# Float32r passes on split operands for the sine half of a dense layer, and the order of the steps around them

## The chip, the cores and the metric

The kernel runs on one core of a Trainium2 chip. The metric is the device time of one execution in microseconds (us). The kernel before takes 1928.28 us, the median of 3 runs (1928.05 to 1929.04).

## The reference

```python
X = np.fft.fft(x, axis=1)            # x: 8 x 3008 x 256, f32
X = np.fft.fft(X, axis=2)
x = X.real.astype(np.float32).reshape(24064, 256)
h = x @ w_in                         # 256 x 2048
g = h * np.clip(h + 3.0, 0.0, 6.0) / 6.0
out = g @ w_out                      # 2048 x 256
```

A Fourier transform over the sequence and over the features, of which the real part is kept, and then two dense layers with a hard swish between them.

## The kernel before

The Fourier transform over the sequence is done as 3008 = 47 x 64: `stage1` (47) and `stage2` (64) are matrix products with tables. The transform over the features is folded into the weights of the first dense layer. Because the input is real, rows k and -k share their products: with u the cosine half of the first layer and v the sine half, the layer's result is u + v for one row and u - v for its mirror row.

The batch of 8 is worked on in 4 pairs. A pair has 12 chunks of 256 columns (the last of each pair has 194, and 192 in the second layer); the features of the dense layers are taken in 8 groups `fc` of 256. One chunk and one `fc` make a step, so there are 4 x 12 x 8 = 384 steps. The first 8 also prepare the weights. The order of all instructions is written out by hand: the loop over steps at the end emits them, and each engine runs its own in that order. `beside` has lists of extra work by step, `ahead` (stage 2, loads, the spreading of a row to all partitions) and `behind` (stage 1).

In a step `s`, the loop emits

- `mlp1` of step s+2. `mlp1_products` (L546) makes four f32 products on TensorE, two for u and two for v, each 128 x 256, into two banks of PSUM. `activate` (L560) follows: on VectorE two operations (L565) add a rank-one term to u and put the sum into s; one makes u = s + v (L575), one v = v - s (L577). ScalarE makes a ReLU of each (L604), and VectorE the product with the upper clip (`gate`, L607) for each. The gated values are in tile a.
- `combine` of step s+1 on GpSimd (L621): sums of parts of a, into c. The second layer uses seven products for a 2 x 2 block product in place of eight.
- every chunk, `finish` (GpSimd) and `store` (transposes on VectorE, L712, and stores on SP's queue) of the chunk before.
- `mlp2` of step s (L651): seven f32 products on TensorE, three on parts of a, then four on c, added over the 8 groups into four banks. At the last group ScalarE copies them out (L661).

`activate_last` is `activate` for the short chunks. PSUM has 8 banks: 4 for the second layer (`ps_a`), 3 for u and v (`ps_h`) and one for the stages (`ps_d`). The tables T of stage 2 (six groups) are all kept in SBUF. `stage2` ends with a copy by ScalarE (L508), `spread` with two DMAs on SP's queue (L515, L516), `stage1` with two copies by ScalarE and DMAs on SP's queue.

Of the kernel before, what the change touches and what calls it, by code (L numbers as in the profile page):

```python
# [12 lines left out]
F16 = mybir.dt.float16  # L13
AL = mybir.AluOpType
# [34 lines left out]
WS = 2.0 ** 20  # L49
N1, N2 = 47, 64  # L50
# [8 lines left out]
def kernel(  # L59
# [41 lines left out]
    gpool = ctx.enter_context(tc.tile_pool(name="gpool", bufs=2))  # L101
    qpool = ctx.enter_context(tc.tile_pool(name="qpool", bufs=3))
# [4 lines left out]
    ps_d = ctx.enter_context(tc.tile_pool(name="ps_d", bufs=1, space=PSUM))  # L107
    ps_h = ctx.enter_context(tc.tile_pool(name="ps_h", bufs=3, space=PSUM))
    ps_a = ctx.enter_context(tc.tile_pool(name="ps_a", bufs=4, space=PSUM))

# [11 lines left out]
    T = consts.tile([P, 2, NG, 2, 2 * KK, N2], F32, name="T")  # L122
# [140 lines left out]
    def bank(shape, name):  # L263
        if starting[0]:
            return ps_a.tile(shape, F32, tag="acc", name=name)
        return ps_d.tile(shape, F32, tag="d", name=name)

    def stage1(pr, c):  # L270
        y = pr.y[c]
        ps = [bank([P, 2, D], "ps1"), ps_h.tile([P, 2, D], F32, tag="uv", name="ps1")]
        for h in range(2):
            last = (c, h) == (NXC - 1, 1)
            for b in range(2):
                n = 1 if last else 2
                nc.tensor.matmul(ps[b][h * PB:(h + 1) * PB, 0:n], F[rows(b), 0:PB], y[rows(b), 2 * h:2 * h + n],  # L277
                                 start=True, stop=not last, skip_group_check=last)
# [93 lines left out]
    def stage1_quarters(hb, m):  # L372
        y = hb.y.pop(m)
        cosine, sine = slice(0, P + 1), slice(P + 1, D)
        ps = [bank([P, 2, D], "ps1"), ps_h.tile([P, 2, D], F32, tag="uv", name="ps1")]
# [65 lines left out]
    def both_tables(gr, blk, u, tab=None):  # L441
        if tab is not None:
            return tab[:, gr, blk, u]
        t = T[:, :, gr, blk, 2 * u]
        (p, b, k), step = t.ap, T[:, 0, gr, blk, 2 * u:2 * u + 2].ap[1][0]
        return bass.AP(t.tensor, t.offset, [p, [b[0] + step, b[1]], k])
# [26 lines left out]

    def spread_half(hb, gr):
# [6 lines left out]
        nc.sync.dma_start(out=first.qn[vg][:, cs], in_=qd[:, cs].to_broadcast([P, TB]))  # L481
        del hb.g[gr]

    def spread_by_pe(hb, ps, tab, copy=nc.scalar.copy):
# [4 lines left out]
        copy(first.qn[0][:, 0:TB], ps)  # L489
        del hb.g[0]  # L490

    def stage2(pr, gr, i, copy=nc.scalar.copy):
# [5 lines left out]
        for u in range(2):  # L498
# [4 lines left out]
            for blk in range(2):  # L503
# [3 lines left out]
                                 T[:, :, gr, blk, kk, 0:nk], start=True, stop=True)  # L507
# [3 lines left out]
    def spread(pr, gr):  # L511
# [4 lines left out]
        nc.sync.dma_start(out=pr.qn[gr][:, 0:n], in_=qd[:, 0:n].to_broadcast([P, n]))  # L516
        del pr.g[gr]

    class Chunk:
# [3 lines left out]
        def __init__(self, pr, ck):  # L523
# [7 lines left out]
            self.a, self.c, self.acc = {}, {}, {}  # L531
# [28 lines left out]
    def activate(ch, fc, u, v, between=None):  # L560
# [11 lines left out]
        if ch.last:  # L572
            activate_last(a, t, s, u, v, nq)
            return
        nc.vector.tensor_tensor(u[:], s[:], v[:], op=AL.add)  # L575
        relu(t[:, 0], u[:], 1.0 / 6.0)
        nc.vector.tensor_tensor(v[:], v[:], s[:], op=AL.subtract)  # L577
# [8 lines left out]
    def activate_last(a, t, s, u, v, nq):  # L586
        un, vn, sn, tn = u[:, :, 0:nq], v[:, :, 0:nq], s[:, :, 0:nq], t[:, :, :, 0:nq]
        nc.vector.tensor_tensor(un, sn, vn, op=AL.add)
        relu(tn[:, 0], un, 1.0 / 6.0)
        nc.vector.tensor_tensor(vn, vn, sn, op=AL.subtract)  # L590
        relu(tn[:, 1], vn, -1.0 / 6.0)

        def slots(x, n, i):
            return x[:, i * P:i * P + 2 * n].rearrange("p (b k) -> p b k", b=2)

        gate(a[:, 0, :, 0:P], tn[:, 0, :, 0:P], u[:, :, 0:P])
        for f in range(2):
            gate(slots(a[:, 0, f], N2 // 2, 1), *(slots(x, NH, 1)[:, :, 0:NH - 1] for x in (t[:, 0, f], u[:, f])))
        for f in range(2):
            gate(slots(a[:, 1, f], N2, 0)[:, :, ::-1], *(slots(x, N2, 0) for x in (t[:, 1, f], v[:, f])))  # L600
            gate(slots(a[:, 1, f], N2 // 2, 1)[:, :, ::-1], *(slots(x, NH, 1)[:, :, 1:NH] for x in (t[:, 1, f], v[:, f])))

# [22 lines left out]
    def mlp2_first(ch, fc, halves=(0, 1)):  # L625
        a = ch.a[fc]
        for h in halves:
# [5 lines left out]
            if fc == NF - 1:  # L633
                if h == 0:
                    ch.r = epool.tile([P, 2, 2, TB], F32, tag="r", name="r")
# [3 lines left out]
    def mlp2(ch, fc):  # L639
        a = ch.a.pop(fc)[:].rearrange("p m f n -> p (m f) n")[:, :, 0:ch.n]  # L640
        c = ch.c.pop(fc)
        moving = [a[:, 0], a[:, 1], a[:, 3], c[:, 0], c[:, 1], c[:, 2], c[:, 3]]
        order = list(enumerate(moving))
        if ch.final and fc == NF - 1:

            order[5:] = order[:4:-1]
        for i, mv in order:
# [5 lines left out]
            if fc == NF - 1 and (i % 2 == 1 or i == 6):  # L653
                if i == 1:
                    ch.e = epool.tile([P, 8, TB], F32, tag="e", name="e")
# [7 lines left out]
    def finish(ch):  # L663
# [4 lines left out]
        r = epool.tile([P, 2, 2, TB], F32, tag="r", name="r")  # L668
# [9 lines left out]
    def finish_final(ch):  # L678
# [3 lines left out]
        ch.r = epool.tile([P, 2, 2, TB], F32, tag="r", name="r")  # L682
# [165 lines left out]
    def load_t(gr):  # L848
        nc.sync.dma_start(out=T[:, :, gr].rearrange("p b a k n -> p b (a k n)"), in_=c_stage2[gr])
# [147 lines left out]
    def beside(p):  # L997
# [7 lines left out]
        if p == 0:  # L1005
            for gr in range(2, NG):
                put(gr if gr < NSG else gr + 8, load_t, gr)
            for gr in range(2):
                put(14 + gr, load_t, gr)
# [23 lines left out]

        def s2(t, pr, gr):
            for i in range(2):
                put(t + 3 + 4 * i, stage2, pr, gr, i)
            put(t + 8, spread, pr, gr)
# [5 lines left out]
        if p + 1 < NP:  # L1043
            nx = pairs[p + 1]
            for c in range(NXC):
# [4 lines left out]
                put(t + 8, stage1, nx, c, at=behind)  # L1050
            put(NST * (NG - 1) - 2, load_g, nx, 0)
# [4 lines left out]
    def close_w():  # L1056
        nonlocal epool
        wctx.__exit__(None, None, None)
        epool = ctx.enter_context(tc.tile_pool(name="epool", bufs=2))

    epool = None
    steps = [(p, ck, fc) for p in range(NP) for ck in range(NCK) for fc in range(NF)]
    AHEAD = 2
# [100 lines left out]
    for s, (p, ck, fc) in enumerate(steps):  # L1164
# [12 lines left out]
        else:  # L1177
            if s + AHEAD < len(steps):
                mlp1(*chunk(s + AHEAD))
            for f, a in behind.get(ck * NF + fc, ()):  # L1180
                f(*a)
# [7 lines left out]
            mlp2(*chunk(s))  # L1189
# [5 lines left out]
def _tables(B, S, D):  # L1195
# [49 lines left out]
    t[0, -1], t[1, -1] = 1.0, (-1.0) ** np.arange(N2)  # L1245
    h = D // 2
# [47 lines left out]
```

## Time and profile before

| | |
|---|---|
| median of 3 runs | 1928.28 us |
| span of the profiled execution | 1926.0 us |
| TensorE busy (PE) | 1912.2 us, 99% |
| weight loads (PEld) | 1653.3 us, 86% |
| VectorE (DVE) | 1432.2 us, 74% |
| ScalarE (ACT) | 678.0 us, 35% |
| GpSimd (POOL) | 1447.7 us, 75% |
| granted TensorE clock | full in all 40 slices |

The profile is of one execution; its instructions and transfers are shown with times from the start of the span. The page has the busy time of each engine, and the chain of waits: the work that ended last, followed back through what released each piece of it. A timeline lists instructions in order of time, equal neighbours merged: start, time from the first start to the last end, engine, line, operation, out<-in, shape, count, and in brackets the idle time before with what ended it. A row by line gives the count, the busy time and the mean time of one. One f32 product on TensorE is two instructions in the profile, each with a weight load of its own. A matmul's record lasts from its start to its result, so that records of neighbours overlap; the rate is read from starts.

### The profile page before, as it was taken

What the parts mean: (1) busy time and instruction counts of PE and PEld (TensorE: products, weight loads), DVE (VectorE), ACT (ScalarE), POOL (GpSimd) and SP (SyncE); (2) the same over time, 40 slices, a digit from 0 to 9 for tenths busy, and PEclk for the clock granted to TensorE, in tenths of its full rate; (3) what the DMA queues carried; (4) which work ended last, traced back from release to release, by engine and by line L of the source; (5) the groups of instructions that cost most, each with busy time, mean ns of one, the idle gap of its engine ahead of it and who ended that gap; (6) DMA issues with size and microseconds to landing.
All of it is one profiled execution on the core that took longest, in us unless ns stands there. A gap on an engine that the chain in (4) does not pass through costs nothing.

```text
span 1926.0 us, 28448 instructions
## 1 busy us (share of the span) xinstructions
PE 1912.2 (99%) x9456; PEld 1653.3 (86%) x9456; DVE 1432.2 (74%) x2756; ACT 678.0 (35%) x1164; POOL 1447.7 (75%) x1658
## 2 busy tenths in 40 slices
PE   9999999999999999999999999999999999999998
PEld 6688888888988888888898888888899888888887
DVE  8967776777877777777787777777778777777777
ACT  6533333333333333333333333333333333333332
POOL 5697888896688788786678787878676667666765
PEclk9999999999999999999999999999999999999999
DMA  7442222211112212121111121221110101101000
GB/s 264 118 132 54 73 72 65 59 47 43 25 43 70 56 46 55 44 58 39 23 40 50 49 56 44 55 56 44 36 28 20 29 17 28 33 12 29 19 20 20
DMA packets 155258, 99.78 MB, mean 52 GB/s; under 512 B 121776, under 2 KB 135579, under 8 KB 155111
## 3 DMA queue, kind: packets, MB, share of 16 engines
q1 hardware_dynamic: 142854, 60.75, 12.9%
q0 software_dynamic: 11008, 36.63, 6.6%
q8 instruction: 74, 1.21, 0.3%
q10 hardware_dynamic: 1248, 0.59, 0.1%
q14 instruction: 74, 0.60, 0.1%
HBM read 61.44 MB, written 36.79 MB: 51 GB/s over the span
## 4 chain that ended last, share of the span: by engine, by line
PE 94%; POOL 2%; DVE 2%; issue 1%; ACT 1%; DMA 0%; SPq 0%; DVEq 0%; POOLq 0%; ACTq 0%
PE acc L651 56%; PE v L556 16%; PE u L556 16%; PE ps L505 2%; PE acc L631 1%; PE ps L277 1%; POOL c L621 1%; DVE a L607 1%; PE spare L832 0%; POOL xt L176 0%; DMA C<-in_c_dim_dram 0%; DVE s L565 0%; DVE o L712 0%; ACT t L604 0%; PE ps L466 0%
## 5 line engine op out<-in xcount | busy, mean ns | idle before, releaser
L621 POOL TENSOR_TENSOR c<-a 128x512 f32<-128x512 f32 (+1 forms) x375 | 469.6, 1252 | 357.8 <-PE acc L651 302.5
L651 PE MATMUL acc<-c,G 128*128 128x256 f32 (+1 forms) x3008 | 697.2, 375 | 0.1
L604 ACT ACTIVATE t<-u,half 128x512 f32<-128x512 f32 (+1 forms) x384 | 261.1, 680 | 1140.3 <-DVE u L575 1055.6
L651 PEld LDWEIGHTS acc<-c,G 128*128 128x128 f32 x3008 | 565.2, 190 | 71.6 <-POOL c L621 0.5
L565 DVE SCALAR_TENSOR_TENSOR s<-qn,WN,u 128x256 f32<-128x256 f32 (+1 forms) x768 | 330.5, 472 | 337.9 <-PE u L556 334.0
L651 PE MATMUL acc<-a,G 128*128 128x256 f32 (+1 forms) x2256 | 541.6, 376 | 0.0
L651 PEld LDWEIGHTS acc<-a,G 128*128 128x128 f32 x2256 | 421.1, 189 | 73.5 <-issue 20.2
L556 PE MATMUL v<-q,W 127*128 127x256 f32 (+1 forms) x1536 | 389.3, 375 | 1.1 <-DVE a L607 1.1
L556 PE MATMUL u<-q,W 128*128 128x256 f32 (+1 forms) x1536 | 388.0, 375 | 0.0
L607 DVE SCALAR_TENSOR_TENSOR a<-t,u 128x512 f32<-128x512 f32 (+2 forms) x448 | 263.9, 601 | 101.3 <-ACT t L604 97.1
L556 PEld LDWEIGHTS v<-q,W 127*128 127x128 f32 x1536 | 287.9, 190 | 41.7 <-ACT t L604 1.9
L556 PEld LDWEIGHTS u<-q,W 128*128 128x128 f32 x1536 | 285.9, 190 | 36.7 <-issue 2.2
L621 POOL TENSOR_TENSOR c<-c,a 128x256 f32<-128x256 f32 (+1 forms) x375 | 269.0, 717 | 29.4
L621 POOL TENSOR_TENSOR c<-a,c 128x256 f32<-128x256 f32 (+1 forms) x375 | 268.9, 717 | 29.4
L575 DVE TENSOR_TENSOR u<-s,v 128x512 f32<-128x512 f32 x352 | 245.0, 696 | 37.7 <-DVE s L565 1.4
L607 DVE SCALAR_TENSOR_TENSOR a<-t,v 128x512 f32<-128x512 f32 (+1 forms) x480 | 263.7, 566 | 0.5 <-ACT t L604 0.4
L604 ACT ACTIVATE t<-v,half 128x512 f32<-128x512 f32 (+1 forms) x384 | 261.1, 680 | 0.6 <-issue 0.4
L577 DVE TENSOR_TENSOR v<-v,s 128x512 f32<-128x512 f32 x352 | 243.9, 693 | 0.0
L621 POOL TENSOR_TENSOR r<-w,e 128x256 f32<-128x256 f32 (+1 forms) x92 | 88.9, 987 | 3.6
L661 ACT ACTIVATE e<-acc 128x512 f32<-128x512 f32 (+2 forms) x184 | 83.5, 545 | 0.0
L712 DVE STREAM_TRANSPOSE o<-r 128x256 f32<-128x256 f32 (+1 forms) x192 | 72.5, 416 | 0.2
L621 POOL TENSOR_TENSOR w<-w,e 128x512 f32<-128x512 f32 (+1 forms) x46 | 57.6, 1251 | 3.6
(130 smaller groups left out, 779.2 us busy)
## 6 DMA issues: line engine op xcount, KB each, us to landing
out_dram<-o SPq DMA_DIRECT2D x744, 32.0 KB
g<-zd SPq DMA_DIRECT2D x42, 256.0 KB
zd<-z SPq DMA_DIRECT2D x48, 192.0 KB
xt<-in_x_dram POOLq DMA_DIRECT2D x21, 256.0 KB
qn<-qd SPq DMA_DIRECT2D x16, 256.0 KB
st<-in_moe_w_out_dram POOLq DMA_DIRECT2D x7, 512.0 KB
xt<-in_x_dram POOLq DMA_DIRECT2D x17, 192.0 KB
st<-in_moe_w_in_dram POOLq DMA_DIRECT2D x6, 512.0 KB
```

The lines of the kernel that those rows point to most:

```text
L277: nc.tensor.matmul(ps[b][h * PB:(h + 1) * PB, 0:n], F[rows(b), 0:PB], y[rows(b), 2 * h:2 * h + n], start=True, stop=not last, skip_group_c ...
L505: nc.tensor.matmul(ps[:, blk, u * P:n].rearrange("p (b k) -> p b k", b=2), g[:, kk, blk * (P + 1):blk * (P + 1) + P], T[:, :, gr, blk, kk, ...
L556: nc.tensor.matmul(ps[:, i, 0:nq], W1[r, blk, f * P:(f + 1) * P], q[r, blk, of:of + nq], start=True, stop=True)
L565: nc.vector.scalar_tensor_tensor(s[:, i, 0:nq], qn[:, of:of + nq], WN[:, f:f + 1], u[:, i, 0:nq], op0=AL.mult, op1=AL.add)
L575: nc.vector.tensor_tensor(u[:], s[:], v[:], op=AL.add)
L577: nc.vector.tensor_tensor(v[:], v[:], s[:], op=AL.subtract)
L604: nc.scalar.activation(t, h, AF.Relu, bias=half[:], scale=scale)
L607: nc.vector.scalar_tensor_tensor(dst, t, 1.0, h, op0=AL.min, op1=AL.mult)
L621: (eng or nc.gpsimd).tensor_tensor(out, in0, in1, op=AL.add)
L651: nc.tensor.matmul(ch.acc[i // 2][:, i % 2, 0:ch.n], G[:, i, fc, :], mv, start=(fc == 0 and i % 2 == 0), stop=(fc == NF - 1), skip_group_c ...
L661: nc.scalar.mul(ch.e[:, k:i + 1, 0:ch.n], ch.acc[i // 2][:, 0:i + 1 - k, 0:ch.n], 1.0 / WS)
L712: nc.vector.transpose(o[:, 0:n // DH, h], ch.r[:, m, h, 0:n].rearrange("p (j i) -> p j i", i=DH))
```

## The change

It touches the steps from 13 on (the first 16 activations stay as they were, but for a constant factor).

- *Operands in three parts.* The sine half of the layer is no longer an f32 product. `split` makes from x three float32r parts: high (x scaled and rounded on ScalarE), low = x - high and rest = (1 + EPS) high - x (VectorE). `split_w` does it once for the weights (steps 8 to 11, into KW). `split_q` does it for the moving operand once a chunk, when step s+3 is the first of its chunk.
- *Six passes.* `odd_half` makes for each of the two 128-column blocks three float32r matmuls: two add onto the bank u of the cosine half, one goes to bank v.
- *The activation.* ScalarE copies v to y in SBUF; VectorE makes u = (1 + EPS) u + y and then v = u - 2 (1 + EPS) s; the ReLUs and gates follow as before. The cosine tables and the spread row carry a factor 1 / (1 + EPS) that this takes back; ScalarE scales the spread row once it has landed.
- *Order.* The first layer runs three steps ahead in place of two, and is cut into parts. Per step: `even_half` (s+3), `first_gate` (s+2), `keep_even` (s+3: s = rank-one term + cosine half, read from bank u), `second_gate` (s+2), `combine` (s+1), `finish` or `store`, the three a products of `mlp2` (s), `odd_half` (s+3), stage 1 if any, the four c products of `mlp2` (s).
- *Memory.* From step 13 PSUM has two banks of kind a (u) and two of kind y (v) besides the four of `ps_a`; stage 2 takes one of kind y, stage 1 one of each. T has one buffer and is loaded group by group. Tiles r and e have one buffer.

The core of the diff:

```diff
+    def split_q(ch):
+        of, nq, q = ch.ck % 2 * TB, ch.nq, ch.pr.q[ch.ck // 2][:, 1]
+        k = qpool.tile([P, 3, TB], F32R, tag="k", bufs=2, name="k")
+        ch.k = k
+        split(k[:, 0, 0:nq], k[:, 1, 0:nq], k[:, 2, 0:nq], q[:, of:of + nq])
+
+    def split(high, low, rest, x):
+        nc.scalar.mul(high, x, 1.0 - EPS / 2.0)
+        h = high.bitcast(F32)
+        nc.vector.tensor_tensor(low, x, h, op=AL.subtract)
+        nc.vector.scalar_tensor_tensor(rest, h, 1.0 + EPS, x, op0=AL.mult, op1=AL.subtract)
+
+    def even_half(ch, fc):
+        of, nq, q = ch.ck % 2 * TB, ch.nq, ch.pr.q[ch.ck // 2]
+        if fc == 0:
+            split_q(ch)
+        u = ps_u.tile([P, 2, TB], F32, tag="a", name="u")
+        for i in range(2):
+            f = 2 * fc + i
+            nc.tensor.matmul(u[:, i, 0:nq], W1[:, 0, f * P:(f + 1) * P], q[:, 0, of:of + nq],
+                             start=(i == 0), stop=True, skip_group_check=True)
+        ch.front[fc] = [u]
+
+    def keep_even(ch, fc):
...
+        for i in range(2):
+            f = 2 * fc + i
+            nc.vector.scalar_tensor_tensor(s[:, i, 0:nq], qn[:, of:of + nq], WN[:, f:f + 1], u[:, i, 0:nq],
+                                           op0=AL.mult, op1=AL.add)
+
+    def odd_half(ch, fc):
+        nq, (u, s) = ch.nq, ch.front[fc]
+        v = ps_u.tile([P, 2, TB], F32, tag="y", name="v")
+        for i in range(2):
+            fs = slice((2 * fc + i) * P, (2 * fc + i + 1) * P)
+            for j, o in enumerate((u, u, v)):
+                nc.tensor.matmul(o[:, i, 0:nq], KW[:, j, fs], ch.k[:, j, 0:nq],
+                                 start=(j == 2 and i == 0), stop=True, skip_group_check=True)
...
+        nc.scalar.copy(yn, vn)
+        nc.vector.scalar_tensor_tensor(un, un, 1.0 + EPS, yn, op0=AL.mult, op1=AL.add)
         relu(tn[:, 0], un, 1.0 / 6.0)
+        nc.vector.scalar_tensor_tensor(vn, sn, -2.0 * (1.0 + EPS), un, op0=AL.mult, op1=AL.add)
         relu(tn[:, 1], vn, -1.0 / 6.0)
...
     def load_t(gr):
+        T[gr] = tpool.tile([P, 2, 2, 2 * KK, N2], F32, tag="T", name="T")
+        nc.sync.dma_start(out=T[gr][:].rearrange("p b a k n -> p b (a k n)"), in_=c_stage2[gr])
...
-            if s + AHEAD < len(steps):
-                mlp1(*chunk(s + AHEAD))
-            for f, a in behind.get(ck * NF + fc, ()):
-                f(*a)
+            if s < SPLIT:
+                mlp1(*chunk(s + 2))
+                if s == SPLIT - 1:
+                    close_ps()
+            more = SPLIT - 1 <= s < len(steps) - 3
+            if more:
+                even_half(*chunk(s + 3))
+            gates = SPLIT <= s < len(steps) - 2
+            if gates:
+                first_gate(*chunk(s + 2))
+            if more:
+                keep_even(*chunk(s + 3))
+            if gates:
+                second_gate(*chunk(s + 2))
             if s + 1 < len(steps):
                 combine(*chunk(s + 1))
...
-            mlp2(*chunk(s))
+            mlp2(*chunk(s), 0)
+            if more:
+                odd_half(*chunk(s + 3))
+            for f, a in behind.get(ck * NF + fc, ()):
+                f(*a)
+            mlp2(*chunk(s), 1)
```

More of the change, by code (lines that the diff above doesn't have):

```diff
@@ new lines, in split_w @@
+    def split_w(i):
+        cs = slice(i * WB, (i + 1) * WB)
+        low, rest = (spool.tile([P, WB], F32, tag="s", name="part") for j in range(2))
+        split(KW[:, 0, cs], low[:], rest[:], W1[:, 1, cs])
+        nc.scalar.mul(KW[:, 1, cs], low[:], 1.0 / EPS)
+        nc.scalar.mul(KW[:, 2, cs], rest[:], -1.0 / EPS)
+    def even_half(ch, fc):
[8 more added lines that the diff above has]
+        ch.front[fc] = [u]
@@ L646, in mlp2 @@
             order[5:] = order[:4:-1]
+        if part != 0:
+            del ch.a[fc], ch.c[fc]
+        if part is not None:
+            order = (order[:3], order[3:])[part]
         for i, mv in order:
@@ L1005, in beside @@
         if p == 0:
[L1006 to L1009, printed above, removed]
+            for t, gr in ((2, 2), (12, 3), (20, 0), (28, 1), (36, 2), (44, 3), (52, 4), (60, 5)):
+                put(t, load_t, gr)
+            for i in range(FF // WB):
+                put(NF + i, split_w, i)
             put(2, spread_half, halves[0], 1)
@@ L1032, in beside @@
                 put(8 * gr + 28 - (gr == 0), spread_half, hb, gr)
+        else:
+            for gr in range(2, NG):
+                put(NST * (gr - 1) - 8, load_t, gr)
         def s2(t, pr, gr):
+            late = 3 * (p == 0 and gr == NSG)
             for i in range(2):
-                put(t + 3 + 4 * i, stage2, pr, gr, i)
-            put(t + 8, spread, pr, gr)
+                put(t + 3 + 4 * i + late, stage2, pr, gr, i)
+            put(t + 8 + late, spread, pr, gr)
         for gr in range(1 if p > 0 else NSG, NG):
```

105 lines of the change are left out of this document (71 added, 34 removed).

## The prediction, made before the result was known

> **What bounds the kernel now.** First the page: its span, and the chain that ended last.
>
> ```profile
> span 1926.0 us, 28448 instructions
> ...
> PE 94%; POOL 2%; DVE 2%; issue 1%; ACT 1%; DMA 0%; SPq 0%; DVEq 0%; POOLq 0%; ACTq 0%
> PE acc L651 56%; PE v L556 16%; PE u L556 16%; PE ps L505 2%; PE acc L631 1%; PE ps L277 1%; POOL c L621 1%; DVE a L607 1%; PE spare L832 0%; POOL xt L176 0%; DMA C<-in_c_dim_dram 0%; DVE s L565 0%; DVE o L712 0%; ACT t L604 0%; PE ps L466 0%
> ```
>
> TensorE is the chain: 56% in the second layer, 32% in the first, whose halves u and v cost the same. Next the timeline of TensorE over part of a step (a step is one fc of one chunk; start, length, then the group):
>
> ```profile
> 745.89 1.89 PE L651 MATMUL acc<-c,G 128*128 128x256 f32 x8
> 747.62 1.03 PE L556 MATMUL u<-q,W 128*128 128x256 f32 x4
> 748.48 0.38 PE L556 MATMUL v<-q,W 127*128 127x256 f32 x1
> ```
>
> Each product is two instructions. Twelve of them take 748.48 - 745.89 = 2.59 us, 0.216 each without a gap; a step has 22, so 22 x 0.216 = 4.75 us. The other engines fit inside it; VectorE and ScalarE in the same step:
>
> ```profile
> 743.93 0.87 DVE L565 SCALAR_TENSOR_TENSOR s<-qn,WN,u 128x256 f32<-128x256 f32 x2 [0.29 <-PE u L556]
> 744.90 0.70 DVE L575 TENSOR_TENSOR u<-s,v 128x512 f32<-128x512 f32 x1
> 745.51 0.69 DVE L577 TENSOR_TENSOR v<-v,s 128x512 f32<-128x512 f32 x1
> 746.42 0.69 DVE L607 SCALAR_TENSOR_TENSOR a<-t,u 128x512 f32<-128x512 f32 x1 [0.21 <-ACT t L604]
> ```
>
> ```profile
> 745.69 0.69 ACT L604 ACTIVATE t<-u,half 128x512 f32<-128x512 f32 x1 [3.46 <-DVE u L575]
> 746.30 0.69 ACT L604 ACTIVATE t<-v,half 128x512 f32<-128x512 f32 x1
> ```
>
> From these I read the prices of hand-overs: VectorE to ScalarE 745.69 - (744.90 + 0.70) = 0.09; ScalarE to VectorE 746.42 - (745.69 + 0.69) = 0.04; two VectorE operations of 512 columns that do not wait follow at 0.61 (744.90, 745.51). In the kernel before, TensorE is two steps ahead of this chain of about 3 us and never waits for it.
>
> **The change on TensorE.** It removes two sine products per step (four instructions, 0.86 us) and adds six float32r instructions, each with its own weights. The trace has no float32r. Rows by shape and type give its neighbours (the last figure is the mean ns of one; the others serve below):
>
> ```profile
> L604 ACT ACTIVATE t<-u,half 128x388 f32<-128x388 f32 x32 | 18.8, 587 | 79.3 <-DVE u L588 79.3
> ...
> L777 PE MATMUL ex<-PM,FI 128*128 128x512 f16 x20 | 6.2, 382 | 0.1
> ...
> L508 ACT COPY q<-ps 128x388 f32<-128x388 f32 x4 | 1.9, 484 | 6.7 <-PE ps L505 6.7
> ...
> L489 ACT COPY qn<-ps 128x256 f32<-128x256 f32 x1 | 0.4, 373 | 0.0
> ```
>
> An f16 instruction of 512 columns takes 382 ns, an f32 one of 256 columns 0.38 us: an f32 instruction streams its columns twice. If float32r streams once, 256 columns cost what 128 f32 columns cost, loads included. That is stage 2, in the timeline and by line:
>
> ```profile
> 701.84 1.05 PE L505 MATMUL ps<-T,g 128*128 128x128 f32 x8
> 702.74 0.38 PE L556 MATMUL u<-q,W 128*128 128x256 f32 x1
> ```
>
> ```profile
> L505 PEld LDWEIGHTS ps<-T,g x320: 186/192/192, 312.0 to 1811.3; 128*128 128x128 f32 x160
> L505 PE MATMUL ps<-T,g x320: 223/275/377, 312.0 to 1811.3; 128*128 128x128 f32 x152, 128*128 128x66 f32 x8
> ```
>
> Eight in 0.90 us: 0.1125 each, 0.275 from start to result. I take that; the bounds are half of 0.1125 (a pass that costs less than any row of this width) and 0.216 (as the f32 instruction). Six make 0.67 us in place of 0.86, so TensorE's own work falls to 4.75 - 0.19 = 4.56 us a step.
>
> The Trainium skill, page "TensorE: Matmul & The Clock Gate", section "Part 3: Packing small matmuls — row/col tiling" (The mechanism), says that a weight load overlaps a running matmul only where it goes to other rows of the array. By that rule each pass would be load plus stream (a rival, below). The row of L505 does not agree: its loads last 192 ns, and yet load and matmul repeat every 112 ns on the same 128 rows.
>
> **The new loop.** The order of the built program shows what the diff hides. The sine passes of step X+1 add onto bank u, so the first waits until VectorE has read the cosine half (keep_even of X+1). On VectorE keep_even of X+1 stands behind the first gate of X, that behind the difference v of X, that behind the sum u of X. The sum waits for ScalarE's copy of the sine bank, which waits for the six passes of X. And in the built program the difference carries a wait on the first ReLU of X, which reads the same bank u. So from passes to passes everything is serial, one turn per step. Three more rows for its links: the copy of 128x512 on ScalarE, and TensorE starting again after VectorE.
>
> ```profile
> 702.93 0.59 ACT L508 COPY q<-ps 128x512 f32<-128x512 f32 x1 [1.72 <-PE ps L505]
> ```
>
> ```profile
> 23.00 0.69 DVE L801 TENSOR_TENSOR wi<-top,ex 128x512 f32<-128x512 f32 x1 [0.27 <-ACT ex L780]
> ...
> 23.80 0.30 PEld L832 LDWEIGHTS wps<-wi,C 128*128 128x128 f32 x2 [0.99 <-PE wps L832]
> 23.83 0.45 PE L832 MATMUL wps<-wi,C 128*128 128x256 f32 x1 [0.62 <-DVE wi L801]
> ```
>
> TensorE to ScalarE: 702.93 - (701.84 + 1.05) = 0.04. VectorE to TensorE: 23.83 - (23.00 + 0.69) = 0.14. The turn, starting when keep_even ends:
>
> - to TensorE 0.14; five passes 0.56 and the sixth to its end 0.28: 0.98
> - to ScalarE 0.04, copy 0.59: 1.61
> - to VectorE 0.04, sum u 0.70: 2.35
> - to ScalarE 0.09, first ReLU 0.69: 3.13
> - to VectorE 0.04, then difference 0.61 and first gate 0.61 at the rate of unhindered operations: 4.39
> - keep_even, two operations in 0.87: **5.26 us**
>
> TensorE needs 4.56 beside it, so the loop sets the step and TensorE waits about 0.6 us before each set of passes, with the second layer's c products and the next step queued behind. Against 4.75 a plain step gets 0.51 us longer.
>
> **Steps that carry more.** I counted kinds in the built program: of 336 full steps on the new path, 41 begin with the split of q, 42 follow a chunk's end, 42 hold a stage 2 and 24 a stage 1 (overlaps put with the dearer), 187 are plain; 32 more are of the short last chunks.
>
> *Split* (once per chunk). ScalarE's scaling of q stands behind the second ReLU of X; its two VectorE operations stand ahead of the first gate of X. Difference ends 3.17 + 0.70 = 3.87, second ReLU 0.09 + 0.69 to 4.65, scaling 0.37 (L489's row) to 5.02, hand-over 0.04, two operations at 0.40 each (the second of the pair in L565's row starts 0.40 after the first) to 5.86, gate 0.61, keep_even 0.87: 7.34. Against 4.75: +2.59.
>
> *Chunk's end.* ScalarE's copies of the old accumulators stand behind the second ReLU (4.65) in its queue; the third product of the new chunk waits for the second bank's copy (0.59). TensorE would have reached it at 0.14 + 0.67 + 8 x 0.216 + 4 x 0.216 + 4 x 0.216 = 4.27 and gets it at about 5.2; of this some 0.3 is later than the loop: +0.81.
>
> *Stage 2 and stage 1* (for L277, then the next group):
>
> ```profile
> 704.56 1.09 PE L277 MATMUL ps<-y,F 47*64 47x512 f32 x8
> 705.58 0.48 PE L651 MATMUL acc<-a,G 128*128 128x256 f32 x1
> ```
>
> A stage 2 costs 0.90 in both kernels; 4.56 + 0.90 = 5.46 is over the loop, so here TensorE sets the step, 5.65 before: -0.19. A stage 1 costs 1.02; it takes a bank of the u kind, so the next cosine half waits for the end of the first gate (3.78 + 0.69 = 4.47), and then 0.14, 0.86 and the three a products 1.30 stand ahead of the passes: step 6.63 against 5.77, +0.86.
>
> *Short chunks* (194 and 192 columns), TensorE's step and VectorE's operations:
>
> ```profile
> 505.32 0.82 PE L556 MATMUL u<-q,W 128*128 128x194 f32 x4
> ...
> 508.92 0.82 PE L556 MATMUL u<-q,W 128*128 128x194 f32 x4
> ```
>
> ```profile
> 964.27 0.57 DVE L588 TENSOR_TENSOR u<-s,v 128x388 f32<-128x388 f32 x1 [0.46 <-DVE s L565]
> 964.75 0.56 DVE L590 TENSOR_TENSOR v<-v,s 128x388 f32<-128x388 f32 x1
> 965.63 0.69 DVE L607 SCALAR_TENSOR_TENSOR a<-t,u 128x256 f32<-128x256 f32 x3 [0.32 <-ACT t L604]
> 966.23 0.74 DVE L607 SCALAR_TENSOR_TENSOR a<-t,v 128x128 f32<-128x128 f32 x4
> 967.41 0.74 DVE L565 SCALAR_TENSOR_TENSOR s<-qn,WN,u 128x194 f32<-128x194 f32 x2 [0.44 <-PE u L556]
> ```
>
> Step 3.60 before. Loop with passes unchanged: 0.98 + 0.04 + 0.48 + 0.04 + 0.57 + 0.09 + 0.59 + 0.04 + 0.48 + 0.60 + 0.74 = 4.65: +1.05 in 28 steps, and some 3.1 in the 4 that split.
>
> At nothing I cost: the tables of stage 2, now 26 loads on SP's queue in place of 6 (each is asked for steps before its use, when its one buffer is already free, so that the stores behind it do not wait; a late one would show as TensorE waiting for a DMA), ScalarE's scaling of the spread row (its DMAs end before ScalarE, free from 4.65 to 6.3 of a turn, comes to it), the split of the weights in steps 8 to 11, where TensorE still runs two steps ahead, and GpSimd, which gains time.
>
> **The sum.** 187 x 0.51 = 95; 42 x 0.81 = 34; 41 x 2.59 = 106; 42 x -0.19 = -8; 24 x 0.86 = 21; 28 x 1.05 + 4 x 3.1 = 42. Together +290 us on the profiled 1926, so 2216; the median of the runs lies 2.3 above the span (1928.28): I forecast **2218 us**.
>
> **Rivals.**
>
> *TensorE still sets the pace (faster).* If a turn took less than 4.75, TensorE's shorter work would show. One link decides: without the ReLU ahead of the difference, the first gate starts at 3.17 and the turn is 4.65; with the split off the path as well, full steps take at best 4.56: 336 x -0.19 = -64, so 1864 us. For it: VectorE is not full. Against: both waits stand in the built program. Chance 0.04.
>
> *Only the split hurts.* Turn 4.65 (no ReLU link) but splits on the path: -0.10 x 295 = -30, then 41 splits at some 6.4 - 4.75 = 1.7, 70, short steps perhaps +5: about 1973. Chance 0.07.
>
> *Passes longer than stage 2's instructions.* If a pass is paced by its load (0.192 in L505's row), five passes add 0.40 a step: 368 x 0.40 = 147, so 2365; at 0.216 it is +0.6 a step, 2440; two such instructions a pass (float32r handled as f32, so that the change does not do what it says) add 1.9 a step, some 2900. For it: no row shows a float32r load. Against: L505's row. Chance 0.12.
>
> *Load and stream in line.* If a float32r load cannot run beside the pass ahead of it, a pass is 0.19 + 0.11 = 0.30: five add 0.94, 368 x 0.94 = 345, so 2563. L505's row speaks against it. Chance 0.04. It is what the Trainium skill's rule above would give.
>
> *The forecast*: chance 0.72. About 0.01 is left for no change; a difference under 0.2% is about what a measurement of this kernel can't tell from none. So faster 0.04, same 0.01, slower 0.95.
>
> The range: ten hand-overs and rates that I may have 0.02 to 0.03 wrong each make 0.25 a turn, 70 to 90 us; a pass of half 0.1125 takes 0.28 off, 85 us; splits 0.5 shorter 20. From 2100 (below it the first two rivals, 0.11) to 2370 (the load-paced case is inside; above it some 0.08).
>
> **What would show it.** In the changed profile: TensorE's first sine pass waiting for VectorE's keep_even in nearly every step, some 0.6 us, over 200 us in all; VectorE's difference waiting for ScalarE; VectorE waiting some 40 times for ScalarE's k; steps of 5.2 to 5.3 us; passes at 0.11. Wrong if the chain of waits is still nine tenths TensorE, if u's passes do not wait, or if passes come at 0.2 us.

## The result, and the profile after

The changed kernel takes 2305.92 us, the median of 4 runs (2304.23 to 2307.04), beside 1928.16 (1928.05 to 1929.04) for the kernel before: a ratio of 1.1957, 95% interval 1.194 to 1.1974, 378 us slower. The forecast was 2218, the range 2100 to 2370. The direction, the mechanism and the length of a plain step came as forecast; the remaining 88 us did not, and most of them lie in one edit that I had put at nothing.

The page of the changed kernel: its span, the busy shares, the granted clock over the 40 slices, and the chain that ended last.

```profile
span 2304.8 us, 30043 instructions
...
PE 2001.2 (87%) x10192; PEld 1663.3 (72%) x10192; DVE 1454.6 (63%) x2856; ACT 950.4 (41%) x1617; POOL 1451.7 (63%) x1658
...
PEclk9989999899999999999999999999999999999999
...
PE 36%; DVE 33%; ACT 21%; issue 4%; DMA 4%; SPq 2%; ACTq 0%; DVEq 0%; another core or an unknown queue 0%; POOL 0%; POOLq 0%
PE acc L736 14%; ACT t L685 11%; PE u L648 10%; DVE v L656 9%; DVE u L654 9%; DVE s L638 7%; ACT y L653 7%; DVE a L688 6%; PE v L648 4%; PE u L629 4%; DMA qn<-qd 2%; PE ps L522 2%; DMA qd<-q 1%; ACT e L746 1%; DVE k L611 1%
```

The chain was nine tenths TensorE. Now it passes TensorE, VectorE and ScalarE in turn, and none of the three is full (87%, 63%, 41%). That is how this loop of hand-overs looks on the page: no engine is the bound, and the time is in the sum of the links. Two slices have a granted clock below nine tenths; the last section comes back to that. The lines of the loop, passes (L648), copy (L653), sum (L654), ReLU (L685), difference (L656), gate (L688) and keep_even (L638), all stand in the chain.

One turn of the loop, from the timelines of TensorE, VectorE and ScalarE in the changed kernel (start, length, group; in brackets the idle time before it and who ended it):

```profile
1001.17 0.50 PE L648 MATMUL u<-k,KW 128*128 128x256 f32 x2 [0.40 <-DVE s L638]
...
1001.51 0.28 PE L648 MATMUL v<-k,KW 128*128 128x256 f32 x1
...
1001.63 0.40 PE L648 MATMUL u<-k,KW 128*128 128x256 f32 x2
...
1001.86 0.28 PE L648 MATMUL v<-k,KW 128*128 128x256 f32 x1
...
1002.23 0.59 ACT L653 COPY y<-v 128x512 f32<-128x512 f32 x1 [1.77 <-PE v L648]
...
1002.85 0.70 DVE L654 SCALAR_TENSOR_TENSOR u<-u,y 128x512 f32<-128x512 f32 x1 [0.46 <-ACT y L653]
...
1003.59 0.69 ACT L685 ACTIVATE t<-u,half 128x512 f32<-128x512 f32 x1 [0.77 <-DVE u L654]
...
1004.30 0.70 DVE L656 SCALAR_TENSOR_TENSOR v<-s,u 128x512 f32<-128x512 f32 x1 [0.75 <-ACT t L685]
...
1004.91 0.68 DVE L688 SCALAR_TENSOR_TENSOR a<-t,u 128x512 f32<-128x512 f32 x1
...
1005.51 0.86 DVE L638 SCALAR_TENSOR_TENSOR s<-qn,WN,u 128x256 f32<-128x256 f32 x2
...
1006.43 0.38 PE L648 MATMUL u<-k,KW 128*128 128x256 f32 x1 [0.40 <-DVE s L638]
```

Read it as a staircase: where the engine changes, a row begins 0.02 to 0.1 us after the end of the one above it; on VectorE the gate and keep_even each begin 0.08 to 0.09 us before the row above ends. The difference starts at 1004.30, just after the ReLU's end at 1003.59 + 0.69, though its own inputs, s and the sum in u, were ready at 1003.55. From passes to passes it is 1006.43 - 1001.17 = 5.26 us. The waits of the whole run (total us, times, longest) carry the same:

```profile
ACT y L653 <- PE v L648: 648.6, 355, 6.3
...
DVE u L654 <- ACT y L653: 425.8, 368, 10.5
...
DVE v L656 <- ACT t L685: 268.7, 361, 0.8
PE u L648 <- DVE s L638: 217.0, 232, 9.8
...
ACT qn L488 <- DMA qn<-qd: 70.2, 10, 11.5
```

The last row is the one that I had not forecast: at ten of 27 scalings of a spread row (L488) ScalarE stands in its queue, 7 us on average, for a DMA. Two of the ten come before the loop starts (the scalings at 58.09 and 140.07; the first passes are at 151.02), eight within it. One of the ten, on ScalarE and on SP's queue, both of the changed kernel:

```profile
444.15 0.69 ACT L685 ACTIVATE t<-v,half 128x512 f32<-128x512 f32 x1 [0.76 <-DVE v L656]
455.48 0.63 ACT L488 ACTIVATE qn<-qn 128x512 f32<-128x512 f32 x1 [10.64 <-DMA qn<-qd]
456.01 0.57 ACT L653 COPY y<-v 128x512 f32<-128x512 f32 x1
```

```profile
439.70 6.40 SPq L802 DMA_DIRECT2D out_dram<-o  x11
446.20 0.41 SPq L532 DMA_DIRECT2D qd<-q  x1
449.22 0.36 SPq L533 DMA_DIRECT2D qn<-qd  x1
```

The two DMAs of the spread (L532 out, L533 back in) are issued at 446.20 and 449.22, behind eleven stores on SP's queue, and the scaling starts 6.3 us after the second issue. ScalarE had reached the scaling at 444.84, and the copy of the sine bank behind it in the queue, a link of the loop, starts only at 456.01.

### The profile page after: what moved, and what is told of

Read it like the earlier page. It is cut to its first block, busy times and chain, and to the rows that moved or that the text cites. A ratio compares the mean times of both kernels' runs of the same rounds, so it can differ in the third digit from the quotient of the medians.

```text
span 2304.8 us, 30043 instructions
## 1 busy us (share of the span) xinstructions
PE 2001.2 (87%) x10192; PEld 1663.3 (72%) x10192; DVE 1454.6 (63%) x2856; ACT 950.4 (41%) x1617; POOL 1451.7 (63%) x1658
## 4 chain that ended last, share of the span: by engine, by line
PE 36%; DVE 33%; ACT 21%; issue 4%; DMA 4%; SPq 2%; ACTq 0%; DVEq 0%; another core or an unknown queue 0%; POOL 0%; POOLq 0%
PE acc L736 14%; ACT t L685 11%; PE u L648 10%; DVE v L656 9%; DVE u L654 9%; DVE s L638 7%; ACT y L653 7%; DVE a L688 6%; PE v L648 4%; PE u L629 4%; DMA qn<-qd 2%; PE ps L522 2%; DMA qd<-q 1%; ACT e L746 1%; DVE k L611 1%
## 5 line engine op out<-in xcount | busy, mean ns | idle before, releaser
L736 PE MATMUL acc<-c,G 128*128 128x256 f32 (+1 forms) x3008 | 740.8, 392 | 0.0
L736 PE MATMUL acc<-a,G 128*128 128x256 f32 (+1 forms) x2256 | 552.2, 378 | 28.8 <-ACT e L746 28.8
L654 DVE SCALAR_TENSOR_TENSOR u<-u,y 128x512 f32<-128x512 f32 (+1 forms) x368 | 253.2, 688 | 425.8 <-ACT y L653 425.8
L648 PE MATMUL u<-k,KW 128*128 128x256 f32 (+1 forms) x1472 | 331.1, 318 | 217.2 <-DVE s L638 217.0
L653 ACT COPY y<-v 128x512 f32<-128x512 f32 (+1 forms) x368 | 212.1, 576 | 652.4 <-PE v L648 648.6
L648 PEld LDWEIGHTS u<-k,KW 128*128 128x128 f32 x1472 | 238.5, 194 | 316.8 <-DVE s L638 185.7
L656 DVE SCALAR_TENSOR_TENSOR v<-s,u 128x512 f32<-128x512 f32 (+1 forms) x368 | 252.2, 685 | 274.0 <-ACT t L685 268.7
L685 ACT ACTIVATE t<-u,half 128x512 f32<-128x512 f32 (+1 forms) x384 | 260.5, 678 | 302.5 <-DVE u L654 277.0
L685 ACT ACTIVATE t<-v,half 128x512 f32<-128x512 f32 (+1 forms) x384 | 260.5, 679 | 276.6 <-DVE v L656 276.6
L638 DVE SCALAR_TENSOR_TENSOR s<-qn,WN,u 128x256 f32<-128x256 f32 (+1 forms) x736 | 314.8, 469 | 55.8 <-PE u L629 52.5
L688 DVE SCALAR_TENSOR_TENSOR a<-t,u 128x512 f32<-128x512 f32 (+2 forms) x448 | 260.8, 594 | 12.4 <-ACT t L685 12.4
L688 DVE SCALAR_TENSOR_TENSOR a<-t,v 128x512 f32<-128x512 f32 (+1 forms) x480 | 262.6, 563 | 0.1
L648 PE MATMUL v<-k,KW 128*128 128x256 f32 (+1 forms) x736 | 210.7, 286 | 0.0
L648 PEld LDWEIGHTS v<-k,KW 128*128 128x128 f32 x736 | 144.0, 196 | 0.0
```

The source lines that it names most:

```text
L638: nc.vector.scalar_tensor_tensor(s[:, i, 0:nq], qn[:, of:of + nq], WN[:, f:f + 1], u[:, i, 0:nq], op0=AL.mult, op1=AL.add)
L648: nc.tensor.matmul(o[:, i, 0:nq], KW[:, j, fs], ch.k[:, j, 0:nq], start=(j == 2 and i == 0), stop=True, skip_group_check=True)
L653: nc.scalar.copy(yn, vn)
L654: nc.vector.scalar_tensor_tensor(un, un, 1.0 + EPS, yn, op0=AL.mult, op1=AL.add)
L656: nc.vector.scalar_tensor_tensor(vn, sn, -2.0 * (1.0 + EPS), un, op0=AL.mult, op1=AL.add)
L685: nc.scalar.activation(t, h, AF.Relu, bias=half[:], scale=scale)
```

## The experiments

My theory: three things add up, the loop over four engines (5.26 us a step), the splitting of q inside that loop, and the row scaling on ScalarE; the float32r passes themselves are a saving. The rivals: the passes or the splitting cost by themselves; one of the three hides the others; or another link stands right behind each one taken away. Every time below but one has beside it the ratio to the kernel before, run on the same chip.

### The splitting one step earlier

```
     def even_half: -  if fc == 0: split_q(ch)
     the loop:      second_gate(*chunk(s + 2))
                    +  if more and s + 4 < len(steps) and chunk(s + 4)[1] == 0:
                    +      split_q(chunk(s + 4)[0])
                    +  (and once at s == SPLIT - 2, for the first chunk)
```

> The changed kernel, but the split of q is issued one step earlier, behind the second gate, so that its two VectorE operations no longer stand ahead of the first gate. Theory (the split lies on the loop): steps with a split fall from 7.18 us to that of a plain one, 5.26, in 45 chunks, so about -86 us: near 2220. Rival (the wait only moves, since the same two operations then stand ahead of the sum u): within 15 us of 2306.

Measured: 2227.41 us (2225.58 to 2229.24), ratio 1.1552 (1.1529 to 1.1575), 78.5 below the changed kernel. VectorE's waits for ScalarE's scaling of q in the changed kernel, then in this run:

```profile
DVE k L611 <- ACT k L609: 52.3, 45, 2.4
```

```profile
DVE k L611 <- ACT k L609: 16.8, 4, 5.3
```

45 waits become 4. A step with a splitting falls from 7.18 to 5.87 us (medians, counted from one set of passes to the next); it does not fall to 5.26, since VectorE's two operations still stand in its queue.

### The sum kept in SBUF

```
-  nc.vector.scalar_tensor_tensor(un, un, 1.0 + EPS, yn, ...)
-  relu(tn[:, 0], un, 1.0 / 6.0)
-  nc.vector.scalar_tensor_tensor(vn, sn, -2.0 * (1.0 + EPS), un, ...)
+  nc.vector.scalar_tensor_tensor(yn, un, 1.0 + EPS, yn, ...)
+  relu(tn[:, 0], yn, 1.0 / 6.0)
+  nc.vector.scalar_tensor_tensor(vn, sn, -2.0 * (1.0 + EPS), yn, ...)
```

The sum goes to tile y, the ReLU and the first gate read it there, and the difference no longer reads the bank that the ReLU reads.

> The changed kernel, but the sum u goes to the tile y in SBUF instead of back to its PSUM bank, and ReLU, difference and first gate read it there; the difference then has no wait on the first ReLU. Theory (the ReLU is a serial link of the loop): a plain step falls by the 0.61 us of the difference, from 5.26 to about 4.65, also where a split or a short chunk is: about -175 us, near 2130. Rival (another link takes its place, or the accumulation as such is what costs): above 2270.

Measured: 2289.95 us (2289.1 to 2290.81), ratio 1.1876 (1.1852 to 1.19), only 16 less. My expectation fell. The wait did go; the operations grew. VectorE and GpSimd in one turn of this run:

```profile
1608.94 0.69 DVE L654 SCALAR_TENSOR_TENSOR y<-u,y 128x512 f32<-128x512 f32 x1 [1.19 <-ACT y L653]
1609.74 0.79 DVE L656 SCALAR_TENSOR_TENSOR v<-s,y 128x512 f32<-128x512 f32 x1
1610.49 1.16 DVE L688 SCALAR_TENSOR_TENSOR a<-t,y 128x512 f32<-128x512 f32 x1
```

```profile
1609.24 0.73 POOL L702 TENSOR_TENSOR c<-c,a 128x256 f32<-128x256 f32 x1
1610.06 1.05 POOL L702 TENSOR_TENSOR c<-a,c 128x256 f32<-128x256 f32 x1
```

The difference follows the sum without a ReLU between them. But the difference and the first gate now read both inputs from SBUF, beside GpSimd's sums, and last 0.79 and 1.16 us where they lasted 0.70 and 0.68; GpSimd's third sum lasts 1.05 instead of 0.72. Over the run the difference has a median of 0.89 us (0.70 where GpSimd is idle), and the first gate one of 1.21. The median plain step stays at 5.29; the turn shown took 5.19. The Trainium skill, page "SBUF — State Buffer", section "SBUF: two separate sides", says that VectorE with two SBUF inputs and a GpSimd operation that reads SBUF take one pair of ports as an exclusive lock, and the later one waits. If so, the lengthening must go where GpSimd does not read; that is the next run.

### The same, without GpSimd's three sums

```
-  add(cn[:, 0:2], ...); add(cn[:, 2], ...); add(cn[:, 3], ...)
+  eng.memset(cn, 0.5)
```

in `combine`, on top of the edit above: GpSimd writes c with a constant in every step and reads nothing for it. What it does once a chunk (`finish`) and for the stages stays.

> As the run with the sum kept in SBUF, but GpSimd's three sums a step into c are left out: it writes c with a constant instead, reading nothing. Theory (there the round stayed at 5.29 us only because VectorE's operations with both inputs in SBUF stand behind GpSimd's): the difference falls from 0.89 to about 0.70 us, the first gate from about 1.2 to about 0.69, a plain step to 4.65 to 4.8, the whole to 2090 to 2150 us. Rival (another link of the round, or two inputs in SBUF by themselves, holds it): plain steps stay above 5.1 and the time at 2250 or more.

Measured: 2158.8 us (2157.39 to 2160.22), ratio 1.1199 (1.1176 to 1.1221). The groups of VectorE with the sum in SBUF, first with GpSimd's sums and then without (busy us, mean ns of one):

```profile
L688 DVE SCALAR_TENSOR_TENSOR a<-t,y 128x512 f32<-128x512 f32 (+2 forms) x432 | 437.5, 1024 | 1.7
L656 DVE SCALAR_TENSOR_TENSOR v<-s,y 128x512 f32<-128x512 f32 (+1 forms) x368 | 336.6, 915 | 38.9 <-PE acc L736 0.9
```

```profile
L688 DVE SCALAR_TENSOR_TENSOR a<-t,y 128x512 f32<-128x512 f32 (+2 forms) x432 | 303.7, 715 | 0.3
L656 DVE SCALAR_TENSOR_TENSOR v<-s,y 128x512 f32<-128x512 f32 (+1 forms) x368 | 273.0, 742 | 39.3 <-DVE y L654 0.9 <-PE acc L739 0.5
```

The means fall from 1024 to 715 and from 915 to 742 ns, and the plain step to 4.65 us, from 5.29. Beside the `memset`, which only writes, the medians are 0.70 and 0.69 us. So the lengthening came from GpSimd's reading, as the page's rule has it, and the link "difference waits for the ReLU" is worth about 2306 - 2159 = 147 us. It may be worth more: some 40 differences and some 40 first gates still last about 1.1 and 1.75 us here, nearly all of them beside the sums of `finish`, which GpSimd still makes.

### The changed kernel itself, without GpSimd's three sums

The same `memset`, on the changed kernel.

> The changed kernel itself, with GpSimd's three sums a step left out in the same way (c is a constant). Theory (in the changed kernel the difference and the first gate read a PSUM bank, so GpSimd does not slow them, and the round is not GpSimd's): plain step 5.2 to 5.26 and 2270 to 2306 us. Rival (GpSimd slows the round here too): plain step below 5.0 and below 2230 us.

Measured: 2302.42 us, one run, beside 1927.87 for the kernel before. 3.5 us less, with turns of 5.25. Where the difference and the first gate read a PSUM bank, GpSimd's sums cost them nothing (the difference lasts 0.70 us in the changed kernel whether GpSimd works beside it or not), and of the 147 us above at most these 3.5 are GpSimd's.

### No scaling of the spread rows

```
-  scale_row(first.qn[vg][:, cs])     (and the same in spread)
+  WNS = WN / (1 + EPS), once; keep_even uses WNS for WN
```

The first two chunks take plain tables and a factor of 1 in their activation.

> The changed kernel, but the factor 1/(1+EPS) of the spread row is put into a scaled copy of the 16 weight columns WN, so that ScalarE no longer waits for the row's DMA; the tables of the first two chunks are left without the factor. Theory (ScalarE stood in its queue for the late row, 70 us in ten places, most of them in the first pair, and the loop with it): the long steps of 8 to 15 us go, as do some 20 us before step 13: -50 to -75, near 2240. Rival (the row is late whoever waits for it, and keep_even then waits as long): within 15 us of 2306.

Measured: 2236.29 us (2234.3 to 2238.28), ratio 1.1598 (1.1575 to 1.1621): 69.6 less, as the theory said. The first of the passes starts earlier; TensorE's groups of u's passes in a stretch at the start, in the changed kernel up to 163 us and then in this one up to 146 (least, median and greatest ns, first and last start):

```profile
L648 PE MATMUL u<-k,KW x12: 278/280/775, 151.0 to 162.7; 128*128 128x256 f32 x12
```

```profile
L647 PE MATMUL u<-k,KW x12: 277/280/550, 134.4 to 145.8; 128*128 128x256 f32 x12
```

16.6 us are won before the first set of passes (151.0 against 134.4), where two of the ten waits stand; the other 53 come behind it, with the eight others.

### Splitting and row scaling together

The two edits, the splitting one step earlier and no scaling of the rows, in one kernel.

> The changed kernel with the splitting one step earlier and the scaling of the spread rows gone, both at once; the round over the four engines stays. Theory (the two lie in different steps and add): 2306 - 78 - 70 = 2158, between 2145 and 2175 us. Rival (they hide one another, since both delay the same chunk's first steps): above 2190.

Measured: 2157.13 us (2157.08 to 2157.17), ratio 1.119 (1.1168 to 1.1212): 148.8 less, where 78.5 + 69.6 = 148.1 was the sum. The two do not hide one another.

### All three edits

> The three edits together: split one step earlier, sum u in SBUF, no scaling of the spread row. Theory: the loop's turn is then 4.65 us, about TensorE's own 4.6, and nothing else is on it: plain steps 4.65 to 4.7 against 4.75 before, chunk ends, stage 1 and short chunks still dearer: 1930 to 1965 us. Rival (the three costs overlap, or the loop has a floor of its own): above 2000. That it is clearly faster than the kernel before is not expected.

This run was made before the one without GpSimd's three sums. Measured: 2191.18 us (2189.1 to 2195.43), ratio 1.136 (1.1341 to 1.1379): my expectation fell, and the run is slower than the two edits without the third. The sum in SBUF not only brings nothing beside GpSimd's sums, it costs 34 us more here. The median plain step stays at 5.29. With GpSimd's three sums left out as well:

> The changed kernel with everything undone but the passes on the cosine half's bank: splitting one step earlier, no scaling of rows, the sum in SBUF, and GpSimd's three sums a step left out (c is a constant). Theory (the round's link, the splitting and the row scaling are the whole of the loss, each worth what it was worth alone): 2306 - 147 - 79 - 70 = 2010, between 1990 and 2030 us, plain steps of 4.65. Rival (they overlap, or a further loss stands behind them): above 2050.

Measured: 2001.86 us (2001.3 to 2002.42), ratio 1.0379 (1.036 to 1.0398). 304 us less than the changed kernel; the parts alone make 147.1 + 78.5 + 69.6 = 295. These three are four fifths of the loss of 378. Of the 74 us that remain to the kernel before, the trace places most: once a chunk, 35 times in all, a step takes 6.1 us where a plain one takes 4.64, some 51 us together. In each of them GpSimd's `finish` for the chunk before stands beside the difference and the first gate. VectorE and GpSimd in one such step:

```profile
1132.27 1.11 DVE L653 SCALAR_TENSOR_TENSOR v<-s,y 128x512 f32<-128x512 f32 x1
1133.30 1.75 DVE L685 SCALAR_TENSOR_TENSOR a<-t,y 128x512 f32<-128x512 f32 x1
```

```profile
1132.10 2.41 POOL L702 TENSOR_TENSOR r<-w,e 128x256 f32<-128x256 f32 x2
```

That is the contention of the sum in SBUF once more, from the sums that were not left out. No run leaves out `finish`, so this share is read from the trace and not shown by an experiment.

### One pass left out

```
-  for j, o in enumerate((u, u, v)):
+  for j, o in ((0, u), (2, v)):
```

> The changed kernel with one of its three passes left out (the second of the two on the cosine half's bank; its part of the sum is missing): four matmuls a step instead of six. Theory (the passes lie in the round over the four engines, so each of them is paid in full): a plain step loses 2 x 0.1165 = 0.23 us and falls to about 5.03, the whole by some 60 to 85 us, to 2220 to 2246. Rival (the passes lie beside the round, and only the hand-overs set it): plain steps stay at 5.26 and the time above 2290.

Measured: 2224.6 us (2221.93 to 2227.27), ratio 1.1534 (1.1513 to 1.1555), 81 less. Two turns of its timeline, the first pass of each:

```profile
1003.21 0.39 PE L648 MATMUL u<-k,KW 128*128 128x256 f32 x1 [0.41 <-DVE s L638]
...
1008.24 0.39 PE L648 MATMUL u<-k,KW 128*128 128x256 f32 x1 [0.41 <-DVE s L638]
```

A turn of 5.03 in place of 5.26: two instructions fewer, 0.23 us less. TensorE waits 0.4 us in either case, and yet fewer passes shorten the step in full: the passes are a link of the loop.

### All passes on the sine half's own bank

```
 mlp1_products (before's order of steps, before's activation, passes for the one f32 product):
+  for j in range(3):
+      nc.tensor.matmul(ps[:, i, 0:nq], KW[r, j, f * P:(f + 1) * P], ch.k[r, j, 0:nq], start=(j == 0), stop=(j == 2))
 activate:
+  nc.vector.scalar_tensor_tensor(un, vn, 1.0 + EPS, sn, op0=AL.mult, op1=AL.add)
+  nc.vector.scalar_tensor_tensor(vn, vn, 1.0 + EPS, sn, op0=AL.mult, op1=AL.subtract)
```

Three passes for each of the two column blocks on the same operands, no row to scale, the banks of PSUM shared out as in the kernel before, and `split_q` for chunk(s + 3).

> The three sine passes all add into the sine half's own bank v, where the one f32 matmul stood; the steps and the activation go in the order of the kernel before, the factor 1 + EPS goes into VectorE's two operations, the splitting stands one step earlier than in the changed kernel, and no spread row is scaled. Theory (what costs the time is the bank of the cosine half as the target, with the round over four engines that it makes, and the placing of splitting and scaling; the passes themselves are a saving): six passes at about 0.1165 us for two f32 products at about 0.43 take 0.17 us or so off TensorE's step, so a plain step goes from 4.75 to about 4.6, the 42 splits cost VectorE and ScalarE some 1 us each where they are felt: 1870 to 1900 us, below 1928. Rival (the passes or the splitting cost by themselves, whatever bank they go to): 1928 or more, with plain steps above 4.75.

Measured: 1939.71 us (1938.48 to 1943.49), ratio 1.0069 (1.0052 to 1.0085). Against the theory, in part: 366 us less than with the passes on u's bank, but above the kernel before. A plain step was 4.59 us, as expected; the splits were the rest:

```profile
PEld v L571 <- DVE k L619: 42.8, 43, 1.3
PE v L571 <- DVE k L619: 34.1, 43, 1.1
```

TensorE now waits for the third part of k, 43 times, and these steps are about 1.1 us longer than their like. The splitting one step earlier (`chunk(s + 4)`):

> As the run with all three passes on the sine half's own bank, but the splitting stands one step earlier still, two steps ahead of its first pass. Theory (there a plain step took 4.59 us, 0.16 less than before, and only the 50 steps with a splitting took about 1.1 us more, since TensorE waited for the third part of k): these steps lose most of that, the plain ones stay, 1939.7 - 50 x 1.1 = 1885, between 1880 and 1905 us, below the kernel before. Rival (VectorE, 79% busy there, cannot take the splitting's two operations beside a step in any place, or k comes as late): 1925 or more.

Measured: 1889.69 us (1889.26 to 1891.3, 5 runs), ratio 0.9801 (0.9787 to 0.9814): faster than both kernels, by 2.0% than the kernel before and by 18% than the changed one. Its chain and part of a step:

```profile
PE 85%; DVE 7%; POOL 3%; ACT 2%; issue 1%; DMA 1%; SPq 0%; DVEq 0%; ACTq 0%; POOLq 0%
```

```profile
1002.03 1.03 PE L574 MATMUL u<-q,W 128*128 128x256 f32 x4
1002.71 1.07 PE L571 MATMUL v<-k,KW 127*128 127x256 f32 x6
1003.61 1.46 PE L741 MATMUL acc<-a,G 128*128 128x256 f32 x6
```

TensorE is most of the chain again and waits for nobody here. Six passes take the place of two f32 products, the steps are 0.16 us shorter (4.59 for 4.75), and the steps with a splitting are like the others (4.60). So neither the passes nor the splitting of q cost time by themselves on this kernel. What costs is what this run takes back together: the passes' target bank, with the order of the steps, the activation and the sharing of PSUM that go with it. No run changes the bank alone; that the bank is the root of it rests on the loop above, whose first link is the passes' wait for `keep_even`'s reading of bank u.

## Why the prediction was right, and where it was wrong

**The loop: right.** 5.26 us forecast, 5.26 measured. The signs named ahead came too: the first pass waits for keep_even 232 times, 217 us in all, and VectorE 45 times for k. The wait is 0.40 us by the records, which last until a matmul's result; by the rate it is 1006.43 - (1004.57 + 6 x 0.216) = 0.56, where some 0.6 was forecast. Link by link from the end of keep_even (1000.64 + 0.47 = 1001.11, first row of that turn on VectorE, below): the last pass ends after 1.03 (0.98 forecast), the copy 1.71 (1.61), the sum 2.44 (2.35), the ReLU 3.17 (3.13), the first gate 4.48 (4.39), keep_even 5.26. The tenth that the passes and the copy's start took more came back at keep_even, which starts 0.08 before the gate's end.

```profile
1000.64 0.47 DVE L638 SCALAR_TENSOR_TENSOR s<-qn,WN,u 128x256 f32<-128x256 f32 x1
```

**The pass: right within 4%.** 0.1125 us taken from stage 2's rows; in the turn above, the second pass on v starts 0.35 after the first, three passes later: 0.117 each. The load of each pass lasts 0.19 us on the same 128 rows, so a load does run beside the pass ahead of it. By that the trace speaks against the rule of the Trainium skill that the prediction weighed (page "TensorE: Matmul & The Clock Gate", section "Part 3: Packing small matmuls — row/col tiling").

**The difference waits for the ReLU: right, and the largest of the three parts of the loss,** 147 us by the run with the sum in SBUF and without GpSimd's three sums. There a plain step is 4.65, the number that the first rival gave for a loop without that link. What the rival overlooked is that its cheapest realisation, the sum in SBUF, brings a contention of its own.

**The kinds of steps: right.** Medians with a splitting 7.18 (forecast 7.34), with a stage 2 5.42 (5.46), with a stage 1 6.70 (6.63), at a chunk's end 5.44 (4.75 + 0.81 = 5.56), in the short chunks 4.61 (4.65). The 78.5 us won by an earlier splitting are three quarters of the 106 that I had booked for it; the rest goes with its operations, which stay in VectorE's queue.

**"At nothing I cost ... ScalarE's scaling of the spread row": wrong, this is the step that failed.** I wrote that its DMAs end before ScalarE comes to it. In ten of 27 cases they do not: they are issued behind other DMAs on SP's queue (eleven stores in the case shown), go out to memory and back, and ScalarE stood at the scaling up to 11.5 us, and up to 10.6 us with the loop's copy behind it. Without the scaling the time is 69.6 us less. With that term the forecast would have been 2218 + 70 = 2288. The error is one of the question: I asked when ScalarE has room, not when the data of an instruction at the head of its queue arrive.

**The other items at nothing.** The split of the weights in steps 8 to 11 was not free: at the start of step 12's second layer the changed kernel is about 14 us behind the kernel before, of which 7 were there at step 8. The 7 go with the row scaling: without it the run is level at step 8 (-0.1 us). Of the other 7, about 5 are there also in the run with all passes on the sine half's own bank and the early splitting, which has the splitting of the weights and otherwise the order of the kernel before (0.1 us behind at step 8, 5.2 at step 12). That nearly closes the account. The run without the scaling is 11.1 us behind at step 13 and 306.5 at its end, so the steps from 13 on cost 295 us, where the sum had 290. The sum over the steps was right within 2%; what it lacked was the scaling (70 us) and the start (some 11). The table loads were rightly put at nothing: no wait of TensorE for a table stands among its waits. GpSimd likewise (3.5 us).

**The rivals.** "Passes longer" and "load and stream in line" fall by the 0.117 us. "Only the split hurts" falls by the 5.26. "TensorE still sets the pace" (1864) did not hold for this kernel, but the run with the passes on their own bank shows that the saving on TensorE was there to be had: 38 us.

## What to carry to other kernels

Before a product is added onto a bank, ask who else reads that bank: an accumulation that must wait for a reader ties TensorE to the reader's queue, and what ran two steps ahead becomes a loop whose length is the sum of all its links. In such a loop every instruction on the way round counts in full, as the pass left out did, and a helper put "where the engine is idle" holds up all that stands behind it when its data are late. Here it paid to add onto the own bank, to put the helper (the splitting) two steps ahead of its first use, and to move constant factors into operands that are prepared once.

## What the runs showed of the hardware that was not expected

**Two SBUF inputs on VectorE beside GpSimd.** The same 128 x 512 operation takes 0.70 us with one input in PSUM, or with GpSimd idle or only writing, and with both inputs in SBUF beside GpSimd's sums up to 1.16 in the turn shown and 1.75 beside `finish`. Keeping a value in PSUM was worth 0.2 to 0.5 us an operation here (medians 0.70 against 0.89, 0.68 against 1.21).

**The clock falls with the long waits.** The mean granted clock is 0.964 in the changed kernel, 0.999 before. Stretches of the changed kernel before, during and after the stall at 445 us (us, then busy us of PE, PEld, DVE, ACT and POOL, granted clock, DMA share, GB/s):

```profile
425.00:440.00 15.00, 13.69 (x75) 10.89 (x74) 9.49 (x18) 8.28 (x15) 13.09 (x15) 1.00 0.16 35
440.00:456.00 16.00, 10.00 (x51) 8.29 (x49) 4.81 (x10) 2.48 (x4) 10.33 (x13) 0.89 0.63 150
456.00:470.00 14.00, 9.73 (x36) 8.16 (x37) 7.81 (x15) 4.80 (x9) 4.02 (x4) 0.63 0.10 21
```

1.00, then 0.89, then 0.63: a stall is paid a second time behind it, in slower matmuls (the eight c products at 461.63 last 3.62 us, those at 446.36 ahead of the stall 1.89). The Trainium skill's page "TensorE: Matmul & The Clock Gate", section "Part 1: The HAM clock gate (the "warmup" mystery)", gives half the clock after an idle window of about 3.4 us; the stretch agrees: TensorE is idle for 9.79 us, and the granted clock is 0.5 from 452.6 on, for 13.7 us. But the trace shows more: of the 30 stretches at a clock of 0.5 between the first passes and the last, 22 stand behind a wait of TensorE of only 2.2 to 3.3 us, as in the steps with a splitting. The short waits of every turn do not do it: with splitting and scaling out of the way, and the loop still there, with waits of 0.4 us a turn and 1.0 to 1.3 us once a chunk, the mean was 0.996.
